# Attention by 64-row halves, then a feed-forward layer: u loads behind each chunk's swap, score units four slots apart, output banks copied one by one

## The chip, the cores and the metric

The kernel runs on one core of a Trainium2 chip. The metric is device time in microseconds (us), lower is better. A run's time is a little more than the span of its profile, which goes from the first to the last instruction.

## The reference, cut to what matters

There are B = 8 batches of S = 3008 rows. u and v have D = 256 columns, z has 64.

```python
scores = (1.0 / S) * np.matmul(z, z.transpose(0, 2, 1))
attn = np.maximum(scores, 0.0) ** 2
x = (u * np.matmul(attn, v)).reshape(B * S, D)
h = x @ w_in                                  # 256 -> 2048
out = (h * (1.0 / (1.0 + np.exp(-1.702 * h)))) @ w_out   # 2048 -> 256
```

The score matrix of a batch is symmetric, and the kernel uses that.

## The kernel before, in words

**Tiles.** A batch has 24 key tiles j of 128 rows (the last has 64) and six chunks i of 512 query rows (the last has 448). `attend(b, i)` makes, for chunk i, out-transposed = v-transposed times the squared scores, as two sums of 128 output columns (c = 0 and 1), each in a bank of the accumulator memory, the tile `o`. The result is multiplied by the transposed u (`gate`, L311) and written to `xt`, which the feed-forward layer reads.

**Units.** A score unit (i, jp) is two key tiles by one chunk: two 64-row matmuls into `sc` (L211, two buffers), a relu on ScalarE into `rl` (L223), a square on VectorE into `a` (L237 or L228). A unit below the diagonal is not computed: it is the transpose of one above, made by a DMA transpose that SyncE issues (`tt<-a`, L243). On the diagonal of batches 1 to 7 the unit jp = 2i is computed in full and half of unit 2i + 1 is a DMA transpose of it (`ad<-a`, L230); that unit has only half the columns to compute (L220, L221). Batches 1 to 7 have 42 units each, 35 of them transposed.

**64-row halves and the swap.** For most chunks a step of `attend` is a pair of 64-row matmuls that run beside each other in the two halves of the array: rows TOP (0 to 63) of the tile for one sum, rows LOW (64 to 127) for the other. Steps 0 to 22 do TOP into sum 0 and LOW into sum 1, step 23 the half tile, and steps 24 to 46 the same tiles with the sums exchanged. [...]the exchange (the swap, at step NJ = 24) has to wait until both sums of step 23 are in. That is done by a `nop` on GpSimd (`post`, L83) that waits for step 23, and by `behind`, which lets step 24 wait for the nop. Chunk 5 and the first two chunks of batch 0 work with full 128-row tiles and have no such swap. GpSimd takes its instructions in the order of the program, so the nop stands behind whatever was given to GpSimd earlier.

**What is given to GpSimd.** `load_u` (L181) gives it four DMAs for the u of a chunk, two chunks ahead, as soon as `turn_u` (L188, a transpose on VectorE, `ut<-uq`) has freed one of the two `uq` buffers. The table `TURN` says at which step of a chunk `turn_u` and then `load_u` are placed. In batches 1 to 7 both stand in chunks 1 and 2 and only the turn in chunks 3 and 4; in batch 0 both stand in chunks 0 to 3.

**Order by hand.** All engines run in the order in which the program is written. `take` puts score units ahead of a step. Tables say how many at which step: `TAIL` while the last two blocks of the batch before go through `down64`, `SCHED` during the chunks (`SCHED0` in batch 0). All units of chunk 0 are done in `down64`; chunk 0's own slots hold those of chunk 1, and so on. At step 24 of chunks 0 to 4 stand two units, between step 23 and the swap.

**Feed-forward.** `up_group` (L335, gelu at L343, L344) and `down` (L358). In batches 0 to 6 the last two blocks, k = 4 and 5, go through `down64`: the second product by 64-row halves, a pair of matmuls (L403) for each step, with a swap too. A block has ns = 4 tiles of 128 rows in two banks `yp`, except block 5 of batches 0, 2, 4 and 6, which has ns = 3 tiles in three banks. After the last step all banks are copied to `y` on ScalarE (L415), and ScalarE issues the store (L376). Banks `yp` and `o` share one ring of four (`ps1`), taken in turn.

Of the kernel before, what the change touches and what calls it, by code (L numbers as in the profile page):

```python
# [9 lines left out]
F32 = mybir.dt.float32  # L10
F16 = mybir.dt.float16
P = 128
# [3 lines left out]
def kernel(  # L16
# [13 lines left out]
    AF = mybir.ActivationFunctionType  # L30
    ALU = mybir.AluOpType

    B, S, D = u.shape
# [3 lines left out]
    NJ = (S + P - 1) // P  # L37
# [3 lines left out]
    NCH = (S + CH - 1) // CH  # L41
    CB = CH // P
# [11 lines left out]
    FSC = csc * csc * float(S) * float(S)  # L54

    dve, act, pe, sp, pool = nc.vector, nc.scalar, nc.tensor, nc.sync, nc.gpsimd
# [8 lines left out]
    pw = ctx.enter_context(tc.tile_pool(name="pw", bufs=2))  # L65
# [13 lines left out]
    TOP, LOW, FULL = slice(0, SREM), slice(SREM, P), slice(0, P)  # L79

    def post(last):

        sig = pool.nop()  # L83
        for m in last:
            tc.add_manual_dep(sig.ins, m.ins.name, SYNC, reason="row tiles of one bank")
        return sig

    def behind(sig, m):
        tc.add_manual_dep(m.ins, sig.ins.name, SYNC, reason="row tiles of one bank")
# [34 lines left out]
    def first_zt(g):  # L124
        z2 = ZT["st"][:, g * CB:(g + 1) * CB]
        zp = ps1.tile([P, CB, P], F16, name="zp", tag="ps1")
        for k in range(CB):
            pe.transpose(zp[:, k, :], z2[:, k, :, :], ident)
        zt = ZT[0][:, g * CB:(g + 1) * CB, :].rearrange("d n p -> d (n p)")
        nb = CB if g < NCH - 1 else CB - 1  # L130
        dst = zt[:, :nb * P].rearrange("d (p n) -> d n p", n=nb)
        if g == 0:
            act.activation(dst, zp[:, :nb, :], AF.Copy, scale=1.0)
        else:
            dve.tensor_copy(dst, zp[:, :nb, :])
        if nb < CB:
            dve.tensor_copy(zt[:, nb * P:], zp[:, nb, :])
# [184 lines left out]
    GT, Y = {}, {}  # L322

    def blocks(b):

        return [(i, CH if i < NCH - 1 or b % 2 else LFULL) for i in range(NCH)]
# [41 lines left out]
    def store(b, k, s):  # L368
        i, n = blocks(b)[k]
        ns = n // P  # L370
        r0 = b * S + i * CH
        full = min(n, S - i * CH) // P
        final = b == B - 1 and k == NCH - 1
        if s == ns - 1 or final and s % 2 == 1:
            s0 = s - 1 if final else 0
            act.dma_start(  # L376
                out[r0 + s0 * P:r0 + min(full, s + 1) * P].rearrange("(n p) c -> p n c", p=P),
                Y[b, k][:, s0:min(full, s + 1), :],
            )
        if s == ns - 1 and full < ns:  # L380
            for h_, bb in enumerate((b, b - 1)):
                (act if b == B - 1 else pool).dma_start(
                    out[bb * S + S0:(bb + 1) * S], Y[b, k][h_ * SREM:(h_ + 1) * SREM, full, :],
                )


    def down64(b, k):

        ns = blocks(b)[k][1] // P
        shift, per = (2, 2) if ns == CB else (1, 1)  # L390
        order = [(s, (s + shift) % ns, ff) for s in range(ns) for ff in range(NFF)]
        turns = [32] if ns == CB else [16, 32]
        last = {s // per: n for n, o in enumerate(order) for s in o[:2]}
        yp, sigs = {}, {}

        def step(n):
            s0, s1, ff = order[n]
            done = []
            for s, h in ((s0, TOP), (s1, LOW)):
                new = s // per not in yp  # L400
                if new:
                    yp[s // per] = ps1.tile([P, 2, D], F32, name="yp", tag="ps1")
                ins = pe.matmul(  # L403
                    yp[s // per][:, s % per, :], GT[b, k, ff // CB][h, ff % CB, s * P:(s + 1) * P], W2[h, ff, :],
                    start=new, stop=n == last[s // per],
                )
                if n in turns:
                    behind(sigs[n], ins)
                done.append(ins)
            if n + 1 in turns:  # L410
                sigs[n + 1] = post(done)
            if n == len(order) - 1:
                y = Y[b, k] = pw.tile([P, CB, D], F32, name="y", tag="y")
                for m in range(ns // per):
                    act.activation(y[:, m * per:(m + 1) * per, :], yp[m][:, :per, :], AF.Copy, scale=1.0 / FSC)  # L415
                store(b, k, ns - 1)

        return turns, [lambda n=n: step(n) for n in range(len(order))]

    LAGY = 2 * NFG + 3  # L420
# [10 lines left out]
    def split(lst, sizes):  # L431
# [8 lines left out]

    TAIL = {1: {n: 1 for n in (3, 12, 44, 54)}, 2: {n: 1 for n in (4, 25, 34, 43)}}
    SCHED = {
        0: {n: 1 for n in (1, 4, 7, 11, 28, 30, 33, 36, 39, 43)} | {NJ: 2},
        1: {n: 1 for n in (4, 9, 34, 40)} | {NJ: 2},
        2: {n: 1 for n in (4, 9, 34, 40)} | {NJ: 2},
        3: {n: 1 for n in (38,)} | {NJ: 2},
        4: {n: 1 for n in (2,)} | {NJ: 2},
# [1 line left out]
    }  # L449


    TURN = {(True, i): 12 for i in range(1, NCH - 1)}
    TURN |= {(False, i): (38, 28)[i] if i < 2 else 12 for i in range(NCH)}

    FIRST_ZT = {3: 3, 11: 4, 19: NCH - 1}
    SCHED0 = {
# [1 line left out]
        1: {0: 2, 8: 2, 15: 2, 22: 2, 30: 2, 38: 2},  # L458
        2: {n: 1 for n in (0, 3, 7, 11, 30, 34, 38, 42)} | {NJ: 2},
        3: {n: 1 for n in (4, 9, 34, 40)} | {NJ: 2},  # L460
        4: {n: 1 for n in (0, 3, 6, 9, 12, 32, 36)} | {NJ: 2},
        5: {0: 1},
    }

    queue = []
# [28 lines left out]
    for b in range(B):  # L494
# [3 lines left out]
        for i in range(NCH):  # L498
            for n, step in enumerate(attend(b, i, b == 0 and i < 2)):
                if b == 0 and i == 0 and n == 5:  # L500
                    load_u(0, 0)
                if b == 0 and i == 0 and n in FIRST_ZT:
                    first_zt(FIRST_ZT[n])
                if n == TURN.get((b > 0, i), -1):
                    k = i + (b > 0)
# [26 lines left out]
        for q in range(head, nup):  # L532
            if more and q in (head + 14, head + 20):
                k = int(q == head + 20)
# [47 lines left out]
```

## Time and profile before

| what | value |
|---|---|
| four runs | 1264.58, 1265.28, 1271.1, 1272.94 us; median 1268.19 |
| the profiled execution: its time, its span | 1264.58 us, 1262.8 us |
| TensorE busy | 1226.4 us, 97% of the span |
| ScalarE busy, VectorE busy, GpSimd busy | 762.9, 622.1, 235.0 us |
| chunk 0 of batch 1, first to last matmul start | 14.32 us |
| chunks 1, 2, 3 of batch 1 | 12.43, 12.96, 10.58 us |

How to read it: PE is TensorE, DVE is VectorE, ACT is ScalarE, POOL is GpSimd, SP is SyncE, PEld are weight loads. "PE o L294 <- POOLq L83" means that the matmuls of line 294 waited for a semaphore that GpSimd's queue raised at line 83. A line of the timeline gives start, length, engine, line, operation, tiles written and read, count, and in brackets the idle time before it with what ended it. All times inside a run count from its span's start.

### The profile page before, as it was taken

To read this page: it belongs to the slowest core of one execution; us is meant where nothing else is said; L and a number is where in the kernel's file an instruction comes from. 1 tells how busy PE (TensorE), PEld (TensorE's weight loads), DVE (VectorE), ACT (ScalarE), POOL (GpSimd) and SP (SyncE) were. 2 spreads that over 40 slices of the span, in tenths; PEclk is the share of its full clock that TensorE was granted. 3 is DMA by queue.
4 is the path that set the end of the run, shared out by engine and by line. 5 is a ranking of instruction groups with operands and counts; after the bars stand their busy time and mean duration, and the time that the engine had idled before them with its cause. 6 is when DMAs were issued, how large, how long until landed. Compare 5 with 4: busy or idle time off the path is not lost.

```text
span 1262.8 us, 24406 instructions
## 1 busy us (share of the span) xinstructions
PE 1226.4 (97%) x10155; PEld 705.8 (56%) x10155; DVE 622.1 (49%) x901; ACT 762.9 (60%) x833; POOL 235.0 (19%) x333
## 2 busy tenths in 40 slices
PE   8999999999999999999999999999999999999998
PEld 3345764466644676446754467444674446744566
DVE  7655445454455445455354554545445454454531
ACT  5667674466735767356673566736666366663763
POOL 5224101221012210123101231003311132000000
PEclk8999999999999999999999999999999999999999
DMA  9936279532896229952297523955339652494011
GB/s 230 179 65 158 81 158 171 96 114 68 165 169 117 93 78 188 147 126 67 89 196 138 122 73 97 203 112 121 101 92 185 115 120 97 105 204 76 1 35 67
DMA packets 370415, 152.08 MB, mean 120 GB/s; under 512 B 312864, under 2 KB 363936, under 8 KB 370304
## 3 DMA queue, kind: packets, MB, share of 16 engines
q1 hardware_dynamic: 311840, 96.38, 38.0%
q0 software_dynamic: 33440, 29.37, 12.1%
q10 hardware_dynamic: 25024, 24.78, 5.8%
q8 instruction: 79, 1.29, 0.5%
q14 instruction: 32, 0.26, 0.1%
HBM read 60.29 MB, written 24.64 MB: 67 GB/s over the span
## 4 chain that ended last, share of the span: by engine, by line
PE 87%; ACT 4%; DVE 2%; POOL 2%; issue 2%; DMA 1%; ACTq 0%; DVEq 0%; SPq 0%
PE o L294 33%; PE hg L335 26%; PE yp L358 19%; PE yp L403 6%; PE sc L211 4%; ACT rl L223 3%; POOL uq L181 2%; DVE ut L188 1%; ACT y L415 1%; DVE a L237 1%; DMA W<-in_moe_w_in_dram 1%; DMA uq<-in_u_dram 0%; ACTq L376 0%; DVE zst L122 0%; DMA zf<-in_z_dram 0%
## 5 line engine op out<-in xcount | busy, mean ns | idle before, releaser
L343 ACT ACTIVATE gf<-hg 128x1024 f32<-128x1024 f32 (+1 forms) x384 | 386.6, 1007 | 208.2 <-PE hg L335 195.8
L223 ACT ACTIVATE rl<-sc 128x1024 f16<-128x1024 f32 x311 | 305.0, 1027 | 239.6 <-PE sc L211 233.7
L344 DVE TENSOR_SCALAR gt<-gf 128x1024 f16<-128x1024 f32 (+1 forms) x384 | 272.6, 711 | 300.2 <-ACT gf L343 298.9
L294 PEld LDWEIGHTS <-V 64*128 64x128 f16 (+1 forms) x4052 | 225.7, 94 | 280.0 <-POOLq L83 29.7
L335 PE MATMUL hg<-xt,W 128*128 128x512 f16 (+1 forms) x1408 | 355.7, 375 | 0.0
L294 PE MATMUL o<-a,V 64*128 64x512 f16 (+2 forms) x2010 | 319.4, 373 | 23.1 <-POOLq L83 17.3
L237 DVE TENSOR_TENSOR a<-rl 128x1024 f16<-128x1024 f16 x276 | 192.0, 696 | 228.6 <-ACT rl L223 227.9
L358 PE MATMUL yp<-W,gt 128*128 128x256 f16 x2176 | 275.4, 273 | 0.0
L358 PEld LDWEIGHTS <-gt 128*128 128x128 f16 x2176 | 212.9, 98 | 70.7
L181 POOL DMA_DIRECT2D uq<-in_u_dram x188 | 125.6, 675 | 643.3 <-DVE ut L188 261.5
L335 PEld LDWEIGHTS <-W 128*128 128x128 f16 x1536 | 150.6, 98 | 121.5 <-issue 1.3
L294 PE MATMUL o<-tt,V 64*128 64x512 f16 (+1 forms) x1762 | 210.1, 376 | 1.5 <-POOLq L83 1.5
L211 PE MATMUL sc<-ZT 64*128 64x512 f16 (+1 forms) x692 | 121.3, 368 | 5.3 <-ACT rl L223 3.5
L403 PE MATMUL yp<-W,gt 64*128 64x256 f16 x1664 | 103.9, 269 | 0.0
L166 POOL CAST V<-vst 128x512 f16<-128x512 f32 x96 | 71.7, 783 | 129.0 <-PE o L294 100.3
L403 PEld LDWEIGHTS <-gt 64*128 64x128 f16 x1664 | 80.4, 94 | 20.0 <-POOLq L83 4.0
L211 PEld LDWEIGHTS <-ZT 64*128 64x128 f16 x692 | 38.9, 94 | 53.9 <-issue 23.9
L311 DVE TENSOR_TENSOR xt<-o,ut 128x512 f16<-128x512 f32 x80 | 51.4, 684 | 19.7 <-PE o L294 19.7
L364 ACT ACTIVATE y<-yp 128x512 f32<-128x512 f32 x68 | 40.5, 595 | 32.7 <-PE yp L358 32.2
L188 DVE STREAM_TRANSPOSE ut<-uq 128x1024 f32<-128x1024 f32 (+1 forms) x48 | 58.4, 1217 | 0.2
L228 DVE TENSOR_TENSOR a<-rl 128x1024 f16<-128x1024 f16 x35 | 24.2, 693 | 66.8 <-ACT rl L223 66.5
L294 PE MATMUL o<-ad,V 64*128 64x512 f16 x280 | 42.8, 376 | 0.0
(31 smaller groups left out, 159.2 us busy)
## 6 DMA issues: line engine op xcount, KB each, us to landing
out_dram<-y ACTq DMA_DIRECT2D x40, 512.0 KB, 2.8
vst<-in_v_dram SPq DMA_DIRECT2D x39, 512.0 KB, 4.7
uq<-in_u_dram POOLq DMA_DIRECT2D x156, 128.0 KB, 2.9
tt<-a SPq DMA_TRANSPOSE x230, 3.4
uq<-in_u_dram POOLq DMA_DIRECT2D x32, 112.0 KB, 4.0
vst<-in_v_dram SPq DMA_DIRECT2D x8, 384.0 KB, 4.4
out_dram<-y ACTq DMA_DIRECT2D x7, 384.0 KB, 3.0
zst<-in_z_dram POOLq DMA_DIRECT2D x7, 368.0 KB, 5.9
```

Source lines behind the costliest of these rows:

```text
L166: pool.tensor_copy(V16[b][:, n0:n0 + VB, k, :].rearrange("p n (q c) -> p n q c", c=QW), vst.rearrange("p n (q k c) -> p n q k c", k=NCC, c ...
L181: eng.dma_start(uq[k * QW:(k + 1) * QW, :n // QW].rearrange("t q k c -> t q (k c)"), src[:, :, cs])
L188: dve.transpose(ut[:, :, :n // QW, :].rearrange("p k q t -> p q k t"), UQ.pop((b, i))[:, :n // QW])
L211: pe.matmul(sc[:, r, :m * P], zt[h, 2 * kp + r, :], zt[h, (qi + 1) * CB - m:(qi + 1) * CB, :], start=True, stop=True,)
L223: act.activation(rl, sc, AF.Relu, scale=csc)
L237: dve.tensor_tensor(a, rl, rl, ALU.mult)
L294: ins = pe.matmul(acc[c][:, :n], V16[b][h, j, c, :], weights(b, i, j)[h], start=(k, m) == first[c], stop=(k, m) == final[c],)
L335: pe.matmul(hg[:, e, :n], W1[:, c, ff * P:(ff + 1) * P], XT[b, i][:, c, :n], start=(c == 0), stop=(c == NCC - 1),)
L343: act.activation(gf[:, :, :n], hg[:, :, :n], AF.Gelu_apprx_sigmoid, scale=1.0 / FSC)
L344: dve.tensor_scalar(g, gf[:, :, :n], FSC, None, ALU.mult)
L358: pe.matmul(yp[:, s % 2, :], GT[b, k, ff // CB][:, ff % CB, s * P:(s + 1) * P], W2[:, ff, :], start=(ff == 0), stop=(ff == NFF - 1),)
L403: ins = pe.matmul(yp[s // per][:, s % per, :], GT[b, k, ff // CB][h, ff % CB, s * P:(s + 1) * P], W2[h, ff, :], start=new, stop=n == last[ ...
```

## The change

Four things, all in the order of the program and none in the arithmetic.

1. `TURN` moves from step 12 to step NJ + 4 = 28 for chunks 1 to 4 of batches 1 to 7 and chunks 2 to 4 of batch 0. With the turn, the u load of chunks 1 and 2 (2 and 3 in batch 0) moves behind the nop of the same chunk.
2. Units of chunk 0 are taken at steps 4, 8, 12, 16, 20, 24 (two), 30, 34, 38, 42 in place of 1, 4, 7, 11, 24 (two), 28, 30, 33, 36, 39, 43. The twelfth moves to chunk 1, whose slots become 4, 10, 16, 24 (two), 34, 40.
3. In batch 0, chunk 4 gets the unit that stood at step 0 of chunk 5, at slots 0, 4, 8, 12, 16, 24 (two), 32, 37, 42.
4. In `down64` the LOW half is issued ahead of the TOP half, which also exchanges the order in which the banks are taken from the ring, and each bank is copied at the step that completes it. With ns = 4 both banks are complete at the last step only; with ns = 3 the bank of tile 1 is complete at step 31 of 48, the others at the last.

```diff
-            for s, h in ((s0, TOP), (s1, LOW)):
+            for s, h in ((s1, LOW), (s0, TOP)):
...
+            for m in yp:
+                if n == last[m]:
+                    if (b, k) not in Y:
+                        Y[b, k] = pw.tile([P, CB, D], F32, name="y", tag="y")
+                    act.activation(Y[b, k][:, m * per:(m + 1) * per, :], yp[m][:, :per, :], AF.Copy, scale=1.0 / FSC)
             if n == len(order) - 1:
-                y = Y[b, k] = pw.tile([P, CB, D], F32, name="y", tag="y")
-                for m in range(ns // per):
-                    act.activation(y[:, m * per:(m + 1) * per, :], yp[m][:, :per, :], AF.Copy, scale=1.0 / FSC)
                 store(b, k, ns - 1)
...
-        0: {n: 1 for n in (1, 4, 7, 11, 28, 30, 33, 36, 39, 43)} | {NJ: 2},
-        1: {n: 1 for n in (4, 9, 34, 40)} | {NJ: 2},
+        0: {n: 1 for n in (4, 8, 12, 16, 20, 30, 34, 38, 42)} | {NJ: 2},
+        1: {n: 1 for n in (4, 10, 16, 34, 40)} | {NJ: 2},
...
-    TURN = {(True, i): 12 for i in range(1, NCH - 1)}
-    TURN |= {(False, i): (38, 28)[i] if i < 2 else 12 for i in range(NCH)}
+    TURN = {(True, i): NJ + 4 for i in range(1, NCH - 1)}
+    TURN |= {(False, i): (38, 28)[i] if i < 2 else NJ + 4 if i < NCH - 1 else 12 for i in range(NCH)}
...
-        4: {n: 1 for n in (0, 3, 6, 9, 12, 32, 36)} | {NJ: 2},
-        5: {0: 1},
+        4: {n: 1 for n in (0, 4, 8, 12, 16, 32, 37, 42)} | {NJ: 2},
+        5: {},
```

## The prediction

> **What bounds the kernel now.** First the page: busy time by engine.
>
> ```profile
> PE 1226.4 (97%) x10155; PEld 705.8 (56%) x10155; DVE 622.1 (49%) x901; ACT 762.9 (60%) x833; POOL 235.0 (19%) x333
> ```
>
> TensorE is busy for 1226.4 of 1262.8 us, so an edit can only gain from the 36 us in which it stands, and somewhat more, because a busy mark lasts past the moment at which the next matmul could start. The view of waits, for TensorE alone, says who holds it:
>
> ```profile
> PE o L294 <- POOLq L83: 18.7, 16, 1.7
> PE sc L211 <- ACT rl L223: 3.5, 4, 0.9
> PE o L294 <- ACT y L415: 3.0, 4, 0.8
> PE o L294 <- DVE a L237: 2.8, 2, 1.8
> ```
>
> Sixteen waits for the swap's nop on GpSimd, four for ScalarE's relu, four for the copy of y, two for a square. Each is an edit's target. Where they are is read from the busy times of stretches; I cut batch 1 at the first and last matmul of chunks 3, 2, 1 and 0 (length, then TensorE busy):
>
> ```profile
> 216.84:227.42 10.58, 10.58 (x102) 4.77 (x100) 4.74 (x7) 2.96 (x3) 0.00 (x0) 1.00 0.41 92
> 203.66:216.62 12.96, 11.29 (x106) 4.98 (x104) 5.94 (x10) 5.61 (x6) 2.52 (x4) 1.00 0.91 169
> 191.02:203.45 12.43, 11.41 (x107) 5.39 (x104) 6.65 (x11) 6.26 (x7) 2.58 (x4) 1.00 0.87 185
> 176.48:190.80 14.32, 13.35 (x120) 6.41 (x117) 7.89 (x13) 11.76 (x16) 0.00 (x0) 1.00 0.92 201
> ```
>
> Chunk 3 has a swap and a nop, no u load, and no idle time: the nop alone is hidden by the two units at step 24. It gives the price of a slot (a pair of matmuls): 46 steps and 3 units after the first, 10.58 / 49 = 0.216 us. Its DMA share is 0.41; in chunks 0 to 2 the 16 DMA engines are at 0.87 to 0.92. The timeline around the swap of chunk 1:
>
> ```profile
> 195.28 1.24 DVE L188 STREAM_TRANSPOSE ut<-uq 128x1024 f32<-128x1024 f32 x1
> 196.63 0.61 PE L211 MATMUL sc<-ZT 64*128 64x512 f16 x4
> 196.81 2.58 POOL L181 DMA_DIRECT2D uq<-in_u_dram  x4 [46.73 <-PE o L294]
> 198.26 2.33 PE L294 MATMUL o<-a,V 64*128 64x512 f16 x20 [1.01 <-POOLq L83]
> ```
>
> The turn ends at 196.5, GpSimd issues four loads of 0.65 us each, the nop behind them is only reached then, and TensorE, ready at 197.1, starts at 198.26. Last, SyncE's queue over chunks 0 to 3:
>
> ```profile
> 183.79 1.22 SPq L230 DMA_TRANSPOSE ad<-a  x1
> 185.11 11.87 SPq L243 DMA_TRANSPOSE tt<-a  x8
> 197.08 1.21 SPq L230 DMA_TRANSPOSE ad<-a  x1
> 198.38 12.28 SPq L243 DMA_TRANSPOSE tt<-a  x8
> 211.51 1.20 SPq L230 DMA_TRANSPOSE ad<-a  x1
> ```
>
> It issues transposes without a break until 210.7, one each 1.35 us (1.26 at work) and up to 3 us while u loads run. It is no bound yet, but it is the second longest chain of these chunks.
>
> [...]LOW follows TOP by 3 to 4 ns, the next pair by 0.109 us (256 columns). [...]Here it halved for 3.41 us at 83.84 after only 2.0 us of waiting (80.92 to 83.14); a stretch inside it reads
>
> ```profile
> 84.00:87.00 3.00, 3.00 (x9) 1.04 (x8) 0.56 (x1) 1.02 (x1) 0.00 (x0) 0.50 0.00 0
> ```
>
> with a clock of 0.50. [...]an `ad` transpose lands 2.3 us after its issue at best, and 4.1 to 5.6 us after it beside the u loads of chunk 2.
>
> **The change, part by part.**
>
> *Turn and u loads behind the swap.* Nothing is added: one turn (1.24 us, VectorE) and four issues (2.6 us, GpSimd) follow the nop. Chunk 1 needs 46 steps and 6 units, 52 slots, 11.23 us; it took 12.43 to 12.47 us in six batches and 13.04 in batch 5, 87.7 in all, so 9.1 us go. Chunk 2 (one of its units is half) needs 51.5 slots, 11.12 us; it took 12.96 and six times 12.42, so 9.6 go. Batch 0, chunks 2 and 3: 13.51 and 12.63 against 11.88 and 11.23, 3.0 go. Together **21.7 us**. Costs: behind the moved turn on VectorE stand the squares of later units, first needed a chunk later; the next nop comes some 42 steps (9 us) later and the loads are issued by then; the loads are needed a chunk or more later. All hidden. Chunk 3's and 4's turns need no load and gain nothing.
>
> *Slots of chunk 0.* ScalarE needs 0.93 us for a relu in a row, 1.02 alone. Units three steps apart come each 4 x 0.216 = 0.86 us and two apart each 0.65, so with two `sc` buffers TensorE must wait; four apart it is 1.08 us. Needed: 46 steps and 11 units' worth, 57 slots, 12.31 us. Measured: 14.32 in batches 1, 3, 5, 7 and 13.98 in 2, 4, 6. Loss 2.01 and 1.67 us. In the odd ones it holds the wait for y:
>
> ```profile
> 177.16 0.96 ACT L415 ACTIVATE y<-yp 128x256 f32<-128x256 f32 x3
> 177.61 0.37 PE L294 MATMUL o<-a,V 64*128 64x512 f16 x1 [0.76 <-ACT y L415]
> ```
>
> *Copies singly.* For ns = 3 the bank that sum 1 takes over is now the one done at step 31, copied 3.5 us before it is wanted; that wait goes. The copy (0.32 us) goes ahead of three relus in `down64`, where ScalarE is full: up to 0.1 us there. ScalarE's rest of the backlog (two copies and 0.5 us for the store) makes the unit at step 12 some 0.3 us late, and in all batches the second unit at step 24 waits 0.2 us for the relu of step 20 (0.43 + 1.02 + 0.05 after its start against 6 slots, 1.29). Left over: 0.6 and 0.2. Gain 4 x 1.4 + 3 x 1.45 = **10 us**. For ns = 4 nothing changes. The moved half unit costs chunk 1 what it saves chunk 0.
>
> *Last unit of batch 0.* At step 0 of chunk 5 it was 2.0 us late (matmul to square 2.2 us). At step 42 of chunk 4 six slots, 1.3 us, are ahead of it: 0.9 us is left, **1.1 us** gained, and with so short a wait the half clock (3.41 us at half speed, **1.7 us**) should go.
>
> *LOW ahead of TOP.* [...]where a unit's TOP, LOW meets LOW, TOP one start lag of 3 ns is lost: 12 places x 2 x 7, 0.5 us at most. No trace shows pairs in this order. Lower bound nothing; upper bound, if pairs ran one after another, 832 x 0.107 = 89 us.
>
> Sum without new waits: 21.7 + 10 + 1.1 + 1.7 = **34.5 us**.
>
> **What becomes late next.** All of this lies in chunks 0 to 2, so TensorE arrives at chunk 3 about 1.45 + 1.2 + 1.3 = 4.0 us earlier in batches 1 to 7, while SyncE's chain of transposes, back to back since `down64`, has no reason to be faster. The half unit of chunk 3's diagonal is wanted at its step 6 (218.13 in batch 1). Its `ad` landed 2.50, 1.32, 1.12, 1.50, 1.96, 0.51, 0.61 us before that (sum 9.5), and could have been issued earlier by 0.77, 0.03, 0.03, 1.44, 0.54, 0.91, 0.63 us, when SyncE was free (sum 4.4). With 7 x 4.0 = 28 us taken away, 28 - 9.5 - 4.4 = **14 us** of wait come back, some 2 us a batch, if the landing stays at its 4.1 to 5.6 us; its place beside the u loads, now issued about 4 us after that unit's matmul, says so. If the loads fall behind it and it lands in 2.3 us, the wait is nothing. Upward: a wait over 2 us may halve the clock again, 1.7 us each, 12 us for seven. I take 13.5: 34.5 - 13.5 = **21 us**. Other transposes: those wanted at step 20 of chunk 2 have 1.8 to 4.1 us of slack against 2.6 us taken away, 0 to 0.8 us in one or two batches; step 20 of chunk 1 has 2.1 or more against 1.45.
>
> **Rivals.**
> 1. *Likeliest: the waits go and the transposes give part back.* Gain 12 to 28 us, 21 in the middle. For it: the unbroken queue and slacks smaller than 4 us in all seven batches. Chance 0.58.
> 2. *The full gain.* The shifted u loads leave SyncE's chain and the `ad` alone, TensorE is never held: 34.5 us, about 1230 to 1234. For it: the next transposes after a load are the slowed ones, and the load moves. Chance 0.27.
> 3. *Most is given back.* Waits of 3 us at step 6 and a halved clock after each: 7 x (3 + 1.7) = 33 us back, 0 to 12 us of gain. Chance 0.11, nearly half of it within 0.5%.
> 4. *Slower: the reversed pair does not overlap.* Place: `down64`, 832 pairs, 0.107 us for each that runs alone. From 28 / 0.107 = 260 of them on, the kernel is slower by over 0.5%; with all, 1247 + 89 = 1336 us. Against it: matmuls of either half look alike in the trace. Chance 0.04.
>
> **How the numbers follow.** The profiled execution took 1264.58 us (span 1262.8 and 1.8 around it), the fastest of the four; 21 off gives 1243.6, and the median, 1268.19, lies 3.6 higher: 1247 us. Low 1231 reaches into the full gain (1230 on the fast run, 1234 on the median); high 1260 is a gain of 8 on the median. A difference of 0.5%, 6.3 us, is about what a measurement of this kernel can tell from none. Faster by more: 0.58 + 0.27 + 0.06 = 0.91; within: 0.05; slower: 0.04.
>
> **What would show it.** Right: the 16 waits for L83 are gone from TensorE's list, no wait for y, chunk 1 near 11.3 and chunk 2 near 11.2 us, chunk 0 near 12.5 and 12.9, clock 1.0 at 84 us, and new waits of 1 to 3 us for the DMA `ad<-a` at step 6 of chunk 3. Wrong: chunk 3 still at 10.6 us (rival 2), clock 0.5 after chunk 3's step 6 (rival 3), pairs of L403 wider than 0.109 us (rival 4), or the nop waiting on GpSimd for something else.

## The result: about 8 us faster in the first measurement, where 21 were forecast

| | before | after |
|---|---|---|
| median of all runs | 1266.19 us (53 runs, 1261.99 to 1286.88) | 1262.76 us (32 runs, 1247.55 to 1281.89) |
| ratio, 95% interval | 1 | 0.9937 [0.9918, 0.9956], 8.0 us less [5.6, 10.4] |
| profiled execution: its time, its span | 1264.58, 1262.8 us | 1247.55, 1245.8 us |
| granted clock of the median run; time lost to the halved clock (time x (1 - clock)) | 0.997; 3.8 us (43 runs beside the first experiments) | 0.991; 11.4 us |

The ratio leaves out runs more than 1.5% above the fastest of the same kernel; for the kernel after, which spreads more, these are 6 of 33, so the medians of all runs differ by less (3.4 us) than the ratio says. Two more measurements of the same program, told below, gave 0.9987 and 0.9962. The gain is small, 0.1 to 0.6%, and in one of the three measurements it cannot be told from none. The forecast was 1247.0 us with a range of 1231 to 1260; the median lies above it. The profiled execution happens to be the fastest of all: it shows what the change can give, and two more profiles below show slower executions. The time lost to the halved clock is an upper measure, because part of a stretch at half clock can pass while TensorE waits (1.4 us of one window in the repeat).

First the chain that ended last in the kernel before, from its page:

```profile
PE 87%; ACT 4%; DVE 2%; POOL 2%; issue 2%; DMA 1%; ACTq 0%; DVEq 0%; SPq 0%
```

Then the page of the kernel after, its rows on the engines' busy time, on the chain that ended last, and on the matmuls fed by `ad`:

```profile
PE 1222.9 (98%) x10155; PEld 726.4 (58%) x10155; DVE 622.8 (50%) x901; ACT 767.2 (62%) x833; POOL 236.9 (19%) x333
...
PE 91%; DMA 4%; ACT 2%; DVE 1%; issue 1%; ACTq 0%; SPq 0%; DVEq 0%
...
L294 PE MATMUL o<-ad,V 64*128 64x512 f16 x280 | 43.1, 379 | 11.0 <-DMA ad<-a 10.9
```

GpSimd (POOL), which had 2% of the chain, has left it, and DMA has gone from 1 to 4%. The third row says where: 11 us of idle TensorE ahead of the matmuls that read `ad`. The view of waits for TensorE (total us, times, longest):

```profile
PE o L294 <- DMA ad<-a: 10.9, 5, 3.3
PE o L294 <- DMA tt<-a: 1.8, 2, 1.0
PE sc L211 <- ACT rl L223: 1.5, 3, 0.7
...
PE o L294 <- DVE a L237: 1.1, 2, 0.8
```

The sixteen waits for the nop at L83 (18.7 us) and the four for y (3.0) are gone from the list; waits for SyncE's transposes took their place. Batch 1 by chunk, 3, 2, 1 and 0, as it was cut for the kernel before (length, TensorE busy; the clock and the DMA share are the columns after POOL's count):

```profile
206.59:217.22 10.63, 10.63 (x102) 5.52 (x100) 4.67 (x7) 2.96 (x3) 1.12 (x2) 1.00 0.63 130
195.26:206.39 11.13, 11.13 (x107) 5.79 (x105) 5.95 (x10) 5.61 (x6) 2.49 (x5) 1.00 1.06 210
183.71:195.06 11.35, 11.35 (x110) 5.95 (x107) 6.76 (x11) 6.79 (x8) 1.09 (x2) 1.00 0.91 179
170.51:183.51 13.00, 12.56 (x119) 6.40 (x116) 7.95 (x12) 11.82 (x15) 0.00 (x0) 1.00 1.02 197
```

Chunks 2 and 1 have no idle time left: 11.13 and 11.35 us in place of 12.96 and 12.43. In this batch chunk 3 is untouched. In batch 2 it is not; its chunk 3, and 2 us after its wait:

```profile
359.78:375.53 15.75, 12.44 (x101) 6.03 (x99) 4.65 (x7) 2.96 (x3) 0.74 (x2) 0.89 0.58 96
...
366.00:368.00 2.00, 2.00 (x14) 0.81 (x10) 0.00 (x0) 0.00 (x0) 0.00 (x0) 0.50 0.04 8
```

15.75 us in place of 10.6: 3.3 us of wait, then a clock of 0.50 for 3.41 us, which costs half of that: there a pair follows the last by 0.427 us, at full clock by 0.216. The timeline of that place (start, length, engine, line; in brackets idle time and what ended it):

```profile
358.01 2.51 POOL L181 DMA_DIRECT2D uq<-in_u_dram  x4 [9.42 <-DVE ut L188]
...
358.54 1.21 SPq L230 DMA_TRANSPOSE ad<-a  x1
...
359.78 1.46 PE L294 MATMUL o<-a,V 64*128 64x512 f16 x12
359.84 4.70 SPq L243 DMA_TRANSPOSE tt<-a  x2
...
364.55 0.61 PE L294 MATMUL o<-ad,V 64*128 64x512 f16 x4 [3.31 <-DMA ad<-a]
```

The square that `ad` copies ended at 356.23. SyncE, with other transposes ahead, issued `ad` at 358.54, 2.3 us late. By then GpSimd had begun to issue the u loads, and `ad` landed only at 364.51, 5.97 us after its issue. TensorE, at step 6 since 361.24, took it 0.04 us later. The same 0.04 us lies between landing and use in all seven batches (in batches 1 and 4 with next to no idle time before it): TensorE now takes `ad` as soon as it lands.

**Accounting.** Of the 34.5 us that the change was to remove, this execution shows 1264.58 - 1247.55 = 17.0. The missing 17.5 lie where the transposes are late: the chunks 3 of batches 1 to 7 took 89.5 us, 15.3 more than 7 x 10.6, and chunk 2 took 1.2 us too long in batch 2 and 1.0 in batch 7. That is 17.5 in all. By cause: listed waits 10.9 (`ad`) and 1.8 (`tt`), and 3.4 for two half-clock windows of 3.41 us; the remaining 1.4 was not traced; idle time that is hidden because a busy mark outlasts the moment at which the next matmul could start would be of this kind (a mark of L294 lasts 0.376 us, and the next pair starts 0.216 us after it).

### The profile page after: what moved, and what is told of

The parts are those of the page before. It is cut to its first block, busy times and chain, and to the rows that moved or that the text cites. A ratio compares the mean times of both kernels' runs of the same rounds, so it can differ in the third digit from the quotient of the medians.

```text
span 1245.8 us, 24406 instructions
## 1 busy us (share of the span) xinstructions
PE 1222.9 (98%) x10155; PEld 726.4 (58%) x10155; DVE 622.8 (50%) x901; ACT 767.2 (62%) x833; POOL 236.9 (19%) x333
## 4 chain that ended last, share of the span: by engine, by line
PE 91%; DMA 4%; ACT 2%; DVE 1%; issue 1%; ACTq 0%; SPq 0%; DVEq 0%
PE o L294 35%; PE hg L335 26%; PE yp L358 19%; PE yp L403 6%; PE sc L211 5%; DMA ad<-a 2%; DMA tt<-a 2%; ACT rl L223 1%; ACT y L416 0%; DVE a L237 0%; DMA zf<-in_z_dram 0%; DVE zst L122 0%; ACTq L376 0%; DVE ut L188 0%; SPq L243 0%
## 5 line engine op out<-in xcount | busy, mean ns | idle before, releaser
L223 ACT ACTIVATE rl<-sc 128x1024 f16<-128x1024 f32 x311 | 309.3, 1024 | 212.4 <-PE sc L211 202.1
L344 DVE TENSOR_SCALAR gt<-gf 128x1024 f16<-128x1024 f32 (+1 forms) x384 | 275.5, 719 | 294.5 <-ACT gf L343 293.2
L294 PEld LDWEIGHTS <-V 64*128 64x128 f16 (+1 forms) x4052 | 243.1, 95 | 258.1 <-issue 27.8
L294 PE MATMUL o<-a,V 64*128 64x512 f16 (+2 forms) x2010 | 315.0, 372 | 1.1 <-DVE a L237 1.1
L294 PE MATMUL o<-tt,V 64*128 64x512 f16 (+1 forms) x1762 | 214.2, 380 | 1.8 <-DMA tt<-a 1.8
L403 PEld LDWEIGHTS <-gt 64*128 64x128 f16 x1664 | 81.0, 94 | 19.4 <-POOLq L83 4.0
L294 PE MATMUL o<-ad,V 64*128 64x512 f16 x280 | 43.1, 379 | 11.0 <-DMA ad<-a 10.9
```

Source lines behind the costliest of these rows:

```text
L223: act.activation(rl, sc, AF.Relu, scale=csc)
L294: ins = pe.matmul(acc[c][:, :n], V16[b][h, j, c, :], weights(b, i, j)[h], start=(k, m) == first[c], stop=(k, m) == final[c],)
L344: dve.tensor_scalar(g, gf[:, :, :n], FSC, None, ALU.mult)
L403: ins = pe.matmul(yp[s // per][:, s % per, :], GT[b, k, ff // CB][h, ff % CB, s * P:(s + 1) * P], W2[h, ff, :], start=new, stop=n == last[ ...
```

## The experiments

Each was timed against the kernel before on the same chip, in 6 to 22 runs. "Faster by" is the median of the kernel before (1266.3 to 1266.9) times (1 - ratio).

### The two halves of the change alone

The first has only the two `TURN` lines of the change, all else as before (the first line is shown); the second is the change with the `TURN` lines of before. In the second the slots, the single copies and the order of LOW and TOP are together; they were not run one by one.

```diff
-    TURN = {(True, i): 12 for i in range(1, NCH - 1)}
+    TURN = {(True, i): NJ + 4 for i in range(1, NCH - 1)}
```

> The kernel before with TURN alone moved to step 28. Theory (SyncE's chain of transposes is not faster, so what TensorE gains ahead of step 6 of chunk 3 beyond some 2 us comes back as a wait for ad there): the swap waits go (21.7 us), TensorE is 2.5 us early at chunk 3 in place of 4.0, so 7 x 2.5 - 13.9 = 4 us come back; no halved clock there or one at most: 16 to 19 us faster, as much as the whole change or more. Rival A (the u loads at their new place slow the transposes): as large a wait at step 6 as in the whole change, about 8 us faster. Rival B (the gains are independent and only scaled down): 0.62 of the whole change, 5 us faster.

> The whole change with TURN back at step 12: slots, banks and the last unit of batch 0 alone. Theory: TensorE is 1.45 us early at chunk 3, less than most slacks there; 10 us of chunk 0 and 2.8 us of batch 0 stay, under 1 us of wait at step 6: 11 to 13 us faster, so that the two halves alone sum to about 30, well over the whole. Rival A: the same 11 to 13. Rival B: 0.38 of the whole, 3 us faster.

Turns alone: 0.9884 [0.9847, 0.9922], faster by 14.7 us, a little less than expected; both rivals lie outside the interval. Slots and copies alone: 0.9950 [0.9926, 0.9973], faster by 6.3, about half of what was expected. The sum of the halves, 21, is far more than both together gave, so the two parts take something from each other. The waits of TensorE, of the first kernel and then of the second:

```profile
PE o L294 <- DMA tt<-a: 9.5, 1, 9.5
...
PE o L294 <- DMA ad<-a: 3.4, 2, 2.3
```

```profile
PE o L294 <- POOLq L83: 18.7, 16, 1.7
PE o L294 <- DMA ad<-a: 2.9, 3, 2.5
PE o L294 <- DMA tt<-a: 1.8, 1, 1.8
```

The waits at L83 stand as before, and merely arriving 1.5 us earlier from chunk 0 already brings the wait for `ad`, with one half-clock window (at 831.5), where under 1 us of wait was expected. Its chunks 3 are 5.1 us too long in all, and 12.8 - 5.1 - 1.8 = 5.9, where 12.8 is the forecast of this half; its profiled execution, 1257.84 us, is 6.7 under that of before. The turns alone showed `ad` waits of 3.4 us in two batches, with one window behind them (at 833.6), and a single wait of 9.5 us for `tt` in batch 0, which stays open (see below).

### `ad` read later

The two `ad` tiles of chunks 1 to 3 go to steps 18 and 19; in chunk 3 that is twelve steps later.

```diff
-            js = js[own:own + 2] + js[own + CB:-CB + 1] + js[own + 2:own + CB] + js[:own] + js[-CB + 1:]
+            js = js[own:own + 2] + js[own + CB:-CB + 1] + js[:own] + js[own + 2:own + CB] + js[-CB + 1:]
```

> The whole change, and in chunks 1 to 3 of batches 1 to 7 the two tiles that need ad are taken at steps 18 and 19, after those that need tt of earlier chunks (chunk 3: 18 in place of 6; chunk 2: 18 in place of 10; chunk 1: 18 in place of 14). Theory: the waits at step 6 of chunk 3 go without anything being made faster, and with them the halved clock; waits of up to 1.2 us for tt at step 20 of chunk 2 stay in some batches: 28 to 33 us faster than before. Rival C (the clock halves for another reason, such as a TensorE that is busier): waits gone but clock still 0.990 and 15 us faster at most.

0.9817 [0.9782, 0.9853], faster by 23.2 us: most, not all, of what was expected. Waits of its profile:

```profile
PE o L294 <- DMA ad<-a: 6.4, 4, 3.1
PE o L294 <- DMA tt<-a: 4.4, 3, 2.3
```

The clock lost in the median run fell to 5.0 us, so rival C is out. The expectation took only the place of one tile to be wrong. But `ad` came later too: in this trace it was issued 1.0 to 3.6 us after its square and landed 3.6 to 7.1 us after its issue, and twelve steps, 2.6 us, were not enough in four batches.

### u loads later: the edit changed nothing

The u load was written further down in the program, in the following chunk.

```diff
+                if b and (i, n) in ((2, 2), (3, 8)):
+                    load_u(b, i + 2)
```

> The whole change, and in batches 1 to 7 each u load is issued in the chunk after its turn (step 2 of chunk 2, step 8 of chunk 3), so that no u load runs beside ad of chunk 3. Theory: SyncE's chain is as long as before, but ad lands some 2.3 us after its issue in place of 4.7; the wait at step 6 shrinks from 2 or 3 us to below 1: 22 to 30 us faster than before. Rival A: all of the wait goes, 30 to 34 us. Rival D (SyncE's issue alone is late, the landing does not matter): no better than the whole change, 8 us.

0.9987 [0.9962, 1.0011]. The order of instructions on every engine, and their waits, came out as in the changed kernel: GpSimd has nothing between the two places, so a later place in the text is no later place in its queue. As an experiment on the loads it failed; as a second measurement of the changed kernel it stands, with 12.7 us lost to the clock in the median run. Its profiled execution took 1267.23 us, near its median of 1265.81. Its waits:

```profile
PE o L294 <- DMA ad<-a: 18.0, 6, 4.6
PE o L294 <- DMA tt<-a: 8.1, 5, 4.3
```

Of the waits for `tt`, 5.3 us lie in batch 0 and 2.9 in batches 1 to 7.

### No u loads beside the transposes

Chunks 4 and 5 of batches 1 to 7 reuse the u of chunks 2 and 3 (the loads of their own u are left out, so the output of these chunks is not the reference's); all else as after the change.

```diff
-                    if k + 2 < NCH:
+                    if k + 2 < NCH and not b:
```

> The whole change without the u loads of chunks 1 and 2 in batches 1 to 7: the u of chunks 4 and 5 is left out and that of chunks 2 and 3 used again. It takes away what runs beside the transposes on the DMA engines, and leaves their number and order. Theory (SyncE's chain is some 1.35 us a transpose by itself, and each u load adds 2 to 4 us to it and 2 to 3 us to a landing): ad of chunk 3 is issued some 5 us earlier and lands in 2.3 to 3 us; no wait at step 6, clock near 1.000 after the start, 28 to 34 us faster than before. Rival (the chain is late by its own issue, u loads or not): waits of over 1 us stay at step 6 in most batches, 15 us faster at most.

0.9733 [0.9708, 0.9759], faster by 33.8 us, about the whole sum of 34.5 that the prediction had without new waits. Waits, and batch 2's chunk 3:

```profile
PE o L294 <- DMA tt<-a: 3.1, 2, 2.3
...
PE o L294 <- DMA ad<-a: 0.3, 1, 0.3
```

```profile
363.03:373.62 10.59, 10.59 (x101) 5.54 (x99) 4.66 (x7) 2.96 (x3) 0.00 (x0) 1.00 0.55 91
```

`ad` of chunk 3 landed 2.3 to 3.2 us after its issue in six batches (4.2 in batch 5), where the changed kernel had 3.3 to 6.0. SyncE needed 12.9 us in the mean from the `ad` of chunk 2 to that of chunk 3, against 14.3. So leaving out the loads makes both the landing and SyncE's chain shorter. SyncE's own count of transposes is the other ingredient, which the next kernel takes.

### Four transposes moved behind `ad`

The transposes of units (1, 8), (1, 9), (2, 8) and (2, 9) are read in chunk 4 only. Here they are issued behind the `ad` of chunk 3; every load and all arithmetic stay.

```diff
+                if b and i in (1, 2) and cj == 4:
+                    late.append(put)
+                else:
+                    put()
```

> The whole change, and the four transposes of units (1,8), (1,9), (2,8), (2,9), which are read in chunk 4 only, are issued behind ad of chunk 3 in place of ahead of it. TensorE's order is untouched and no transfer is left out. Theory: ad of chunk 3 has four transposes fewer ahead of it, 5.4 us at least, tt of step 20 of chunk 2 two fewer, 2.7 us; the waits of 1 to 6 us go, and with them the halved clock: 25 to 33 us faster than before, the best of all versions. Rival (landing beside the u loads is what is late, wherever SyncE stands): waits of 1 to 2 us stay at step 6, 10 to 15 us faster.

0.9768 [0.9724, 0.9811], faster by 29.4 us, with all loads in place. The only wait for a transpose left in its profile, and chunk 3 of batch 2:

```profile
PE o L304 <- DMA ad<-a: 0.9, 1, 0.9
```

```profile
356.46:367.06 10.60, 10.60 (x102) 5.55 (x100) 4.67 (x7) 2.96 (x3) 0.75 (x2) 1.00 1.06 205
```

SyncE's queue in batch 2, first of the changed kernel, then of this one:

```profile
342.92 1.21 SPq L230 DMA_TRANSPOSE ad<-a  x1
344.24 14.20 SPq L243 DMA_TRANSPOSE tt<-a  x8
358.54 1.21 SPq L230 DMA_TRANSPOSE ad<-a  x1
```

```profile
338.00 1.21 SPq L232 DMA_TRANSPOSE ad<-a  x1
339.30 11.50 SPq L249 DMA_TRANSPOSE tt<-a  x6
353.33 1.19 SPq L232 DMA_TRANSPOSE ad<-a  x1
```

In the changed kernel eight transposes stand back to back between the two `ad`. Here there are six, and SyncE is idle from 350.8 to 353.3: it is waiting for data, no longer the bound. The gain is twofold: `ad` is issued 0.06 to 0.41 us after its square (0.8 to 2.5 in the changed kernel), and therefore ahead of the u loads (354.70), so it lands in 2.3 to 3.9 us.

### The clock alone

To tell the wait from the halved clock behind it, eight matmuls on zeros (8 x 0.216 = 1.73 us, result unused) were put ahead of step 6 of chunk 3 in batches 1 to 7; the changed kernel without them ran beside it on the same chip.

```diff
+                if b and i == 3 and n == 6:
+                    fw = ps2.tile([P, 2, CH], F32, name="fw", tag="ps2")
+                    for q in range(8):
+                        pe.matmul(fw[:, 0, :], nil[:, :P], nil, start=(q == 0), stop=(q == 7))
```

> The whole change, and in batches 1 to 7 eight full matmuls on zeros (1.73 us, nobody reads them) ahead of step 6 of chunk 3. They stand where TensorE waits for ad. Theory: a wait over 1.7 us is filled and costs nothing, a shorter one is lengthened, by about 5 us over the run; but the clock does not halve after chunk 3's wait[...], which saves 1.5 us each time: clock 0.995 in place of 0.991, time between 5 us better and 3 us worse than the whole change. Rival (the halved clock has nothing to do with these waits): clock stays at 0.991 and the time is 3 to 8 us worse.

> The changed kernel itself, beside the others on one chip. Expected by every theory: 0.990 to 0.998 of before with a mean clock near 0.991; its scatter from run to run is larger than that of before, because each late transpose costs TensorE directly.

The changed kernel again: 0.9962 [0.9938, 0.9986], median 1265.42 us, 13.3 us lost to the clock in the median run. With the filler: 0.9952 [0.9929, 0.9975], median 1261.27, 5.0 us lost. So 8 us of clock came back by keeping TensorE busy there: the halving follows from these waits. That the time falls by as much is not shown: it fell by 4 us in the medians and by 0.1% in the ratios, within the noise. The waits of the kernel with the filler:

```profile
PE o L294 <- DMA ad<-a: 5.9, 6, 2.3
PE o L294 <- DMA tt<-a: 4.9, 3, 2.8
```

In its trace the chunks 3 of batches 1 to 7 are 21.5 us too long, the filler included, where those of the repeat below are 28.0 too long; but its chunks 2 are 6.6 too long, where those of the repeat are 3.0.

The repeat also has the profile of a slower execution than the first. Its waits, then chunk 3 of batch 6 and a stretch inside it:

```profile
PE o L294 <- DMA ad<-a: 19.1, 7, 4.6
PE o L294 <- DMA tt<-a: 2.6, 2, 2.4
```

```profile
974.34:992.34 18.00, 13.44 (x102) 6.17 (x100) 4.67 (x7) 2.96 (x3) 0.75 (x2) 0.81 0.65 86
979.20:985.60 6.40, 5.22 (x26) 2.21 (x27) 0.00 (x0) 0.00 (x0) 0.00 (x0) 0.50 0.43 69
```

Seven waits of 1.1 to 4.6 us, and 17.1 us at half clock (windows at 211.0, 822.0, 979.0, 1139.4; the third lasts 6.83 us and begins 1.4 us before the wait ends). Its chunks 3 of batches 1 to 7 took 102.2 us, 28.0 more than 7 x 10.6, and its chunks 2 are 3.0 us too long. 34.5 - 28.0 - 3.0 = 3.5; this execution took 1260.15 us, 4.4 under the profiled one of before. The execution of 1267.23 us gives the same sum once batch 0 is counted: its chunks 3 and 2 are 26.1 and 3.4 us too long in batches 1 to 7 and 7.9 in batch 0, and 34.5 - 26.1 - 3.4 - 7.9 = -2.9, where it was 2.7 us slower than the profiled one of before. So one sum holds for three executions over nearly 20 us of scatter, and the scatter is in the late transposes of chunks 2 and 3.

### Is the later order good by itself?

Two controls: the kernel before with those four transposes behind `ad`, and the same with the turns moved too. The best version ran again beside them on another chip.

> The kernel before with the four transposes of units (1,8), (1,9), (2,8), (2,9), read in chunk 4, issued behind the `ad` of chunk 3. Theory (SyncE's chain of transposes is a bound only once the waits for the nop are gone): no more than 4 us of gain (the kernel before has 18.7 us of waits at L83 and hardly any for `ad` or `tt`), chunks 1 and 2 still 12.4 us, chunk 3 10.6. Rival (the later order saves time by itself, whatever the rest of the program does): 20 us or more faster, as far as the changed kernel gained by it.

> The kernel before with the turn and the u loads behind the swap and with the same four transposes issued behind the `ad` of chunk 3; slots and copies as in the kernel before. Theory (turn part 21.7 us, its loss given to SyncE's chain taken away): 20 to 24 us faster than before, no wait for `ad` over 1 us, chunk 3 at 10.6 us; the changed kernel with the same order gained 29 to 31, so the slots and copies are worth 7 to 10 on top. Rival (the turn alone already had its whole gain, the chain takes nothing there): 15 us, as the turn alone.

> The changed kernel with the four transposes issued behind the `ad` of chunk 3, a second time on another chip. Theory (the wait and the halved clocks behind it are gone, so the scatter with them): 29 to 31 us faster than before again, granted clock 0.995 or more in the median run, no wait for `ad` over 1 us. Rival (the first measurement was a lucky one of a kernel without slack): 20 us or less.

On the kernel before: 0.9997 [0.9976, 1.0018], nothing. With the turns: 0.9831 [0.9808, 0.9855], faster by 21.4 us. The changed kernel with it: 0.9758 [0.9727, 0.9790], faster by 30.6. Waits of the first, then of the second:

```profile
PE o L304 <- POOLq L83: 17.7, 15, 1.7
PE o L304 <- DMA tt<-a: 6.7, 1, 6.7
```

```profile
PE o L304 <- DMA tt<-a: 3.8, 2, 3.1
PE sc L213 <- ACT rl L225: 3.5, 4, 0.9
PE o L304 <- ACT y L425: 3.0, 4, 0.8
```

While the nop held TensorE, SyncE's order was worth nothing. With the nop out of the way the turns alone went from 14.7 (9.9 to 19.4, on another chip) to 21.4 (18.4 to 24.3), the forecast 21.7; for the turns by themselves the two intervals just overlap, for the whole change they are far apart. In the kernel with the turns chunk 3 is 10.60 us in batches 1 to 7, and its six runs lie between 1241.60 and 1246.55 us, where the 22 of the repeat of the changed kernel lie between 1251.21 and 1281.64. The scatter was expected to go from the best version too, and it did not go entirely: its runs lie between 1228.78 and 1245.35 us, the second time between 1231.09 and 1241.87. The profile of that second time has one kind of late transpose left, in chunks 2 and 3 of batch 0, which are 6.7 us too long:

```profile
PE o L304 <- DMA tt<-a: 4.9, 2, 3.8
```

| kernel | faster by, as changed | with the four transposes later |
|---|---|---|
| before | 0 | 0.4 |
| turns alone | 14.7 | 21.4 |
| turns, slots and copies | 8.0, 1.6 and 4.8 (three measurements) | 29.4 and 30.6 |

## Why the prediction was wrong, by its own steps

- **Turn and loads behind the swap, 21.7 us: right.** 21.4 measured with SyncE relieved; chunk 1 at 11.35 and chunk 2 at 11.14 us (forecast 11.3 and 11.2) wherever no transpose is late. One slip is small: chunk 3 of batch 0 took 12.42 us before, first to last matmul start, not 12.63, so batch 0 gives 2.8 us in place of 3.0.
- **Slots and copies, 10 us, with 1.1 and 1.7 for batch 0: right in the trace.** Chunk 0 took 12.42 to 12.45 us in the even batches and 12.66 to 13.00 in the odd ones (12.5 and 12.9 forecast). Over batches 1 to 7 that is 10.7 us less than before, of which 0.8 went to chunk 1 with the moved half unit. The last unit of batch 0 is 0.8 us late (0.9 forecast), and the clock at 84 us is 1.0. Between the two kernels with SyncE relieved, on one chip, this part is worth 30.6 - 21.4 = 9.2 us, against 12.8; the intervals of both ratios are 6 us wide and cannot tell these apart.
- **LOW ahead of TOP, nothing: right.** It was an estimate until then. The two blocks of `down64` last 14.8 us in the even batches and 16.4 in the odd ones, first to last matmul start, in both kernels, and a pair takes 0.109 us in both; rival 4 is out.
- **What becomes late next: the right place and mechanism, its size too small.** SyncE's unbroken queue, `ad` of chunk 3, step 6, landing in 4.1 to 5.6 us: it landed in 3.3 to 6.0, and the trace shows eight transposes in 14.20 us without a gap. The wait, taken at 14 us, was 10.9 in the fastest execution and 18.0 and 19.1 in two others: the right place and order of size, too small for most executions.
- **The term that failed is the halved clock behind those waits, and with it the size of the waits.** The prediction named the clock ("1.7 us each, 12 us for seven") and then took 13.5 us for everything, that is nothing for the clock. Two executions nearer the median, of 1260.15 and 1267.23 us, lost 31.0 and 29.5 us in chunks 2 and 3 of batches 1 to 7: 19.1 and 18.0 us of waits for `ad`, 2.6 and 2.9 for `tt`, and in each five windows of 3.41 us at half clock, which cost 8.5 us at most. The clock is the larger miss, 8.5 us where nothing was taken; the waits are 4 to 5 us above the 14 of the forecast. Over all runs the clock says the same: 11.4, 12.7 and 13.3 us lost in the median run of three measurements against 3.8 before. The clock was lost by pricing a mean. "Some 2 us a batch" looks harmless, but the prediction's own slacks, taken batch by batch, give waits of 0.7, 2.7, 2.9, 1.1, 1.5, 2.6 and 2.8 us, and the kernel before had shown a window after a wait of 2.0 us, which was in the text. In the repeat the seven waits spread from 1.1 to 4.6 us, and the four of 2.6 us and more halved the clock.
- **The other transposes, 0 to 0.8 us: too small.** In batches 1 to 7 they cost 1.8, 2.6 and 2.9 us of wait in three profiles of the changed kernel. That batch 0 could be late was not considered; it cost 5.3 us of wait in the third.
- **The chances.** Rival 3, waits of 3 us and a halved clock, 0 to 12 us of gain, had 0.11. It is what most executions do: against the median of before, 28 of the first 33 gained less than 12 us or nothing. The likeliest case, a gain of 12 to 28 us, holds for the other five, among them the profiled one. Rival 2, the full gain, needs a kernel in which SyncE has room: 33.8 and about 30 us were measured there. Its ground, that a moved load may leave the `ad` alone, failed because `ad` was issued so late that it ran beside the loads: between 1.0 us ahead of the first of them and 0.7 us behind it in the profiled execution.

Two things stay open. A wait of 1.8 to 9.5 us for `tt` in chunks 2 or 3 of batch 0 appears in eight of the thirteen profiles, in the control too, whose batch 0 is that of the kernel before (6.7 us); what makes it late was not followed, and it blurs every comparison of single executions. And the experiments do not divide the loss between SyncE's issue and the traffic of the u loads: taking away either removes the wait.

## What to carry to other kernels

When a wait on one queue is removed, write down how much slack the second longest chain has at every point that the faster engine reaches; if it is used up, first shorten that chain, for instance by issuing late what is read late: here that is worth 0.4 us before the change and more than 20 after it. Price the waits that come back one by one, not as a mean, since in this kernel one of 2 us or more can cost a window of 3.41 us at half clock, 1.7 us, on top. Where two chains met with no slack the time scattered (22 runs from 1251.21 to 1281.64 us in the repeat, six from 1228.78 to 1245.35 with the four transposes later), so the profile of one fast execution says what a change can give, not what it gives.

## What the runs showed of the hardware that was not expected

- The length of a wait of TensorE does not decide alone whether the clock halves. It read 0.50 after waits of 2.25 us without u loads, 2.31 with the turns alone, 2.47 with the slots alone, 2.63 and 2.67 in the repeat. Yet 2.31 us (kernel after, batch 5), 2.40 (the repeat) and 3.10 (`ad` read later, batch 2) left it at 1.00. Inside each of the thirteen traces all changes of the clock lie whole multiples of 3.413 us apart (before: 8.74, 83.84 and 1261.43 us are 22 and 345 of them apart; after: 365.43 and 1126.60, 223). So the windows of a trace can be laid out from its own clock changes. Here are a window and the next one of the kernel after (wait of 3.31 us, batch 2), then the two windows that share the wait of 3.10 us with `ad` read later:

```profile
362.02:365.43 3.41, 0.88 (x10) 0.47 (x10) 0.00 (x0) 0.00 (x0) 0.00 (x0) 1.00 0.94 190
365.43:368.85 3.42, 3.42 (x20) 1.50 (x18) 0.00 (x0) 0.00 (x0) 0.00 (x0) 0.50 0.24 53
...
361.31:364.72 3.41, 1.75 (x18) 0.75 (x13) 0.00 (x0) 0.00 (x0) 0.00 (x0) 1.00 0.98 97
364.72:368.13 3.41, 1.98 (x20) 1.03 (x21) 0.00 (x0) 0.25 (x1) 0.00 (x0) 1.00 1.02 167
```

  The first wait leaves TensorE idle for 2.53 us of one window, and the next runs at 0.50. The second is split into 1.66 and 1.43 us, and the clock stays at 1.00. Over all thirteen traces, without the first 15 us but with the end of the run, a window with 2.0 us or more of idle time, by TensorE's busy marks, was followed by half clock in 32 cases of 32. Of 20 windows with 1.5 to 1.9 us one was (1.84 us, before, at 80.4), and with less it happened once (1.41 us, in a window already at half clock). So a wait of one length can cost 1.7 us in one execution and nothing in another, as that of 2.31 us did.
- Beside the u loads `ad` of chunk 3 took microseconds longer to land, and a lead of 1.4 to 1.7 us was mostly enough: with that lead over the first of four u loads (four transposes behind `ad`) it landed in 2.3 us in five batches of seven, and in 3.4 and 3.9 in the others. Issued between 1.0 us ahead of it and 1.8 us behind it, `ad` took 3.3 to 6.4 us (two profiles of the changed kernel).
